# First layer in blocks of 2, 2, 2 and six times 3 chunks instead of eight times 3, with new durations and ranks for the planner of the order

## The chip, the cores and the metric

The kernel runs on one core of a Trainium2 chip. TensorE (PE) multiplies matrices into PSUM, VectorE (DVE) and ScalarE (ACT) work elementwise, SyncE (SP) issues the transfers between HBM and on-chip memory. Each engine takes its own instructions in the order in which they stand. The metric is the device time of one launch in microseconds (us), the median of several runs.

## The reference

A recurrence over time with a complex decay, then two dense layers:

```
scale = min(|a|, 0.999) / (|a| + 1e-6);  A = a * scale        # a complex: a_re, a_im
for t in range(768):                                          # 4 batches x 8 heads, D = 48
    S = A[t] * S + outer(k[t], v[t])                          # S is 48 x 48, complex
    y[t] = q[t] @ real(S)
x = y of all heads, as [3072 tokens, 384]
h = x @ w_in;   x = (max(h, 0) + alpha * min(h, 0)) @ w_out   # 384 -> 2048 -> 384
h = x @ w2_in;  out = (h - tanh(h)) @ w2_out                  # 384 -> 2048 -> 384
```

The weights and alpha arrive as float64; everything else is float32.

## The kernel before

**Recurrence.** The tokens are cut into 24 chunks of 128. Two chunks are a unit, prepared together (`unit`): ScalarE and VectorE form log|A| and its angle, TensorE sums them along the tokens (L623), and sines, exponentials and a Newton step give the factors for q and k. Then each chunk (`chunk`) turns k and q (L715, tile `kqt`), transposes them on TensorE (L726), forms the scores (L736) which VectorE masks (L738), and adds the products with the state (L754) and with v (L755) to y. The product of k and v (L765) is added to the state by VectorE (L774, in the first chunk of a batch L771) and scaled (L776). y is copied and written to HBM (`x0d`, feature by token).

**Layers.** `layer` takes one block of tokens. The first layer's block has 3 chunks, 384 tokens, so there are 8 blocks (`SIZES`, L970). The block is read back in three parts (`xf`, L801) and each part split into a high float32r half (ScalarE, L808) and a low one (VectorE, L811), tile `xt`. Then follow 16 steps of 128 hidden units. A step has 9 products into `h` (L825: three parts of 128 features, each as high by high, high by low, low by high), the activation on ScalarE and VectorE (L832, L835, tile `gg`), its split into `ghi` (ScalarE, L843) and `glo` (VectorE, L845), and 9 products into three accumulators (L856). The block's tokens are the moving columns of all 18. In the second layer (8 blocks of 384 tokens, L839, L841, L858) the activations are the weights of the second product. `h`, `gg`, `ghi` and `glo` have two buffers each, `x` (PSUM of the recurrence) three.

**Weights.** 128 hidden units of float64 weights (`weights`) come into one of two `raw` buffers. ScalarE takes magnitudes (L449), VectorE shifts and joins the words in four instructions (L35, L36, L37, L39), ScalarE copies the high float32r half (L457); the low half comes from VectorE (L472) or, for the nine weights of `PE_LO`, from TensorE by two products with the unit matrix and its negative (L466, L467), copied by ScalarE (L469).

**Order.** Nothing is issued in the order in which the code is written. `Order.add` records each operation with its engine, an estimate of its duration, its tiles and a rank (`want`). `Order.issue` then plays the program forward with these estimates: whenever an engine is free, it takes among the operations that can start by then the one with the lowest rank, if its tiles have a slot. So the durations and ranks set where each instruction stands on its engine, and nothing else; on the chip the engines wait for each other by semaphores. The ranks of the first three units are `U_WANT`, of their second chunks `C_WANT`, of later units `AHEAD` before the block that needs them, of the first layer's weights `W_WANT` (start and step). The steps of layer one have ranks 0, 1, 2, ... from the first block on, 16 to a block.

Of the kernel before, what the change touches and what calls it, by code (L numbers as in the profile page):

```python
# [18 lines left out]
def f64_words(raw):  # L19
    """Low and high words of a tile of float64 bits, the high ones also read as float32."""  # L20
    w = raw.bitcast(I32).rearrange("p (n two) -> p n two", two=2)
    wf = raw.bitcast(F32).rearrange("p (n two) -> p n two", two=2)
    return w[:, :, 0], w[:, :, 1], wf[:, :, 1]


def f64_steps(nc, raw, t):
    """float64 bits (raw(), [P, n] int64) to float32 bits in t() ([P, n] int32), on VectorE;
    t() holds the high words' magnitudes, read as float32, before.

    The high word holds sign, 11 bits of exponent and 20 of mantissa. Magnitudes outside  # L30
    float32's normal range are clamped to its ends, then the exponent's three surplus bits
    are shifted out and the low word's top three bits fill the mantissa."""
# [17 lines left out]
# High words of float64 2**-126 and of float32's largest number, read as float32.  # L50
# [4 lines left out]
def general_attention(tc, q, k, v, a_re, a_im, xd):  # L55
    """The recurrence step by step, any |a|; xd[token, (head, e)] gets y."""
# [131 lines left out]
C = 128          # tokens of a chunk of the recurrence  # L188
UN = 2 * C       # tokens of a unit: two chunks, prepared together
# [8 lines left out]

class Order:
    """Puts the program's operations in the order in which they are issued.  # L200

    An operation names its engine, about how long it takes, the tiles it reads and writes and
    those that it allocates; `want` is the rank by which an engine picks among those that can
    start. Dependences follow from the order in which the operations are added. Only shapes
    enter, so the order is the same for all inputs."""

    # from the end of one operation to the start of another that needs it, by their engines
    HOP = {("act", "dve"): 0.14, ("dve", "act"): 0.13, ("act", "act"): 0.14, ("dve", "dve"): 0.13,
           ("dve", "pe"): 0.26, ("act", "pe"): 0.26, ("pe", "dve"): 0.2, ("pe", "act"): 0.2, ("pe", "pe"): 0.0}
    COLD, WARM_UP = 3.4, 4.0        # TensorE runs at half its rate after such a pause, for that long  # L210
# [6 lines left out]
    def add(self, eng, dur, fn, want, r=(), w=(), new=(), lat=0.0, tab=None, after=()):  # L217
        i = len(self.ops)
        deps, order = set(), set(after)
        for key, tag, *parts in new:  # L220
# [4 lines left out]
            if tag not in self.FREE:  # L225
                # slots are handed out in the order in which operations are added
                if tag in self.last_new:
                    order.add(self.last_new[tag])
                self.last_new[tag] = i
# [22 lines left out]
    def chain(self):  # L252
        """ACT's functions in an order that seldom changes its table."""
# [92 lines left out]
class Fast:  # L346
    """The recurrence by chunks, from running sums of log|A| and of its angle, and the two
    MoE layers. `flag` becomes 1 if all of `a` lies where those sums are exact enough."""
# [27 lines left out]
    # -------------------------------------------------- tiles, and operations by engine  # L376
# [17 lines left out]
    # -------------------------------------------------- constants  # L394
    def constants(self):
# [24 lines left out]
        # what the general path is chosen by: sums and maxima over each unit's rows  # L420
# [5 lines left out]
    # -------------------------------------------------- weights  # L426
    def weights(self, ph, f, want):
        """float64 weights of 128 hidden units to two float32r parts."""
# [46 lines left out]
    def cvtag(self, ph, f):  # L475
        """The slot of a weight's float32 values: one of later weights' while there are some."""
        return CV[ph][f]

    def wtag(self, ph, f):
        """The slot of the weights: the second layer's begin in slots of the recurrence's."""  # L480
# [6 lines left out]
    # -------------------------------------------------- attention  # L487
    def unit(self, u, wants):
        """The running sums of a unit's two chunks. wants: rank of the operations of each chunk."""
# [30 lines left out]
        for p, sl in enumerate(halves):  # L520
# [24 lines left out]
            # logs, then 1/ar and 1/mag roughly  # L545
# [7 lines left out]
            # u = ai / ar: a Newton step on the rough 1/ar  # L553
# [7 lines left out]
            # 2 log|A|, where |A| = mag min(mag, 0.999) / (mag + 1e-6)  # L561
# [16 lines left out]
        if u % self.UPB:  # L578
            # the angle goes on from the unit before
# [3 lines left out]
        # running sums of the chunk's logs, and of the unit's angles in turns  # L583
        for what, src, keys in (("l", "sq1", sq1), ("t", "arc", arc)):
            for c in range(2):
# [15 lines left out]
                if u >= SPLIT:  # L601
# [6 lines left out]
                    dur = 0.163 * len(terms)  # L608
# [59 lines left out]
    def rank(u, what):  # L668
        """The table that ScalarE needs, and the place in the order in which it changes tables:
        each unit by itself at first, then with one unit's steps between another's."""  # L670
# [5 lines left out]
    def chunk(self, u, j, w0):  # L676
# [11 lines left out]
        # |P| = e (1 + (lc - ln e)), and its reciprocal by a Newton step  # L688
# [30 lines left out]
        for half in range(2):  # L719
            for nm in ("q", "k"):  # L720
# [6 lines left out]
                P(w0, 0.43, tr, r=[t], w=[ps], new=[(ps, "x")], after=[self.turn_pe] if half else [])  # L727
# [9 lines left out]
            self.turn_pe = P(w0, 0.86, score, r=[qT, kT], w=[ps], new=[(ps, "x")])  # L737
# [5 lines left out]
        for half in range(2):  # L743
            qT, sc = K("qT", half), K("sc", half)

            def yy(half=half, qT=qT, sc=sc):
                o = self.tile(y, "x", [128, 4, 128], psum=True) if half == 0 else T[y]
                for i in range(4):
                    h = 4 * half + i
                    m = 64 if h % 2 == 0 else D     # all rows up to the last one are written  # L750
# [7 lines left out]
        if not last:  # L758
            # the state after the chunk, in the scale of the next one's start
# [7 lines left out]
            P(w0, 0.64, kv, r=[K("kt"), K("v")], w=[ps], new=[(ps, "x")], after=[self.last_y] if self.last_y else [])  # L767
# [246 lines left out]
```

## Time and profile before

| | |
|---|---|
| timed runs (us) | 1081.90, 1082.46, 1085.41; median 1082.46 |
| profiled execution: span, first to last instruction | 1079.8 us |
| profiled execution's own time outside the span | not recorded; the median is 2.66 us above the span |
| PE busy | 1030.6 us (95%), 6584 products |
| PE weight loads busy | 990.1 us (92%) |
| DVE busy | 694.9 us (64%), 1229 instructions |
| ACT busy | 620.5 us (57%), 1234 instructions |

Times in the trace count from the span's start. A busy time is the union of an engine's instructions. Products are pipelined, so the record of one is longer than the distance to the next; what a product costs in a stream is the distance between starts. The same holds in part for VectorE. A wait is the idle time of an engine before an instruction, put down to the instruction that ended it. A float32 product is recorded as two, a float32r product or a transpose as one.

### The profile page before, as it was taken

To read this page: it belongs to the slowest core of one execution; us is meant where nothing else is said; L and a number is where in the kernel's file an instruction comes from. 1 tells how busy PE (TensorE), PEld (TensorE's weight loads), DVE (VectorE), ACT (ScalarE), POOL (GpSimd) and SP (SyncE) were. 2 spreads that over 40 slices of the span, in tenths; PEclk is the share of its full clock that TensorE was granted. 3 is DMA by queue.
4 is the path that set the end of the run, shared out by engine and by line. 5 is a ranking of instruction groups with operands and counts; after the bars stand their busy time and mean duration, and the time that the engine had idled before them with its cause. 6 is when DMAs were issued, how large, how long until landed. Compare 5 with 4: busy or idle time off the path is not lost.

```text
span 1079.8 us, 17238 instructions
## 1 busy us (share of the span) xinstructions
PE 1030.6 (95%) x6584; PEld 990.1 (92%) x6584; DVE 694.9 (64%) x1229; ACT 620.5 (57%) x1234; POOL 1.2 (0%) x8
## 2 busy tenths in 40 slices
PE   3578999999999999999999999999999999999997
PEld 1356999999999999999999999999999999999996
DVE  5998997986878876778787478843334343433332
ACT  7888679768588684868744356543334342433332
POOL 0000000000000000000000000000000000000000
PEclk9689999999999999999999999999999999999999
DMA  8556443244233333221335024210101010100000
GB/s 177 135 142 169 117 125 111 46 71 106 44 68 73 68 75 73 55 57 38 97 76 174 16 75 148 86 38 7 45 1 45 1 45 1 45 7 23 9 16 25
DMA packets 184466, 73.66 MB, mean 68 GB/s; under 512 B 146468, under 2 KB 180280, under 8 KB 184376
## 3 DMA queue, kind: packets, MB, share of 16 engines
q1 hardware_dynamic: 184376, 72.49, 26.9%
q8 instruction: 53, 0.87, 0.3%
q14 instruction: 37, 0.30, 0.1%
HBM read 58.27 MB, written 14.19 MB: 67 GB/s over the span
## 4 chain that ended last, share of the span: by engine, by line
PE 91%; ACT 5%; DVE 1%; DMA 1%; issue 1%; SPq 0%; ACTq 0%
PE h L825 37%; PE acc L858 19%; PE acc L856 18%; PE x L726 4%; PE x L736 4%; PE x L754 2%; PE x L765 2%; PE x L755 2%; PE x L623 2%; PE acc L623 1%; PE x L466 1%; DMA raw<-in_moe_w_out_dram 1%; ACT L549 0%; ACT w L457 0%; DMA a<-in_a_re_dram 0%
## 5 line engine op out<-in xcount | busy, mean ns | idle before, releaser
L825 PE MATMUL h<-xt,w 128*128 128x384 f32 x2088 | 398.2, 338 | 0.7 <-DVE gg L841 0.5
L825 PEld LDWEIGHTS h<-xt,w 128*128 128x128 f32 x2088 | 364.9, 188 | 3.1 <-issue 1.3
L845 DVE TENSOR_TENSOR glo<-gg,ghi 128x384 fp32r<-128x384 f32 x256 | 142.0, 555 | 109.8 <-ACT ghi L843 109.5
L856 PE MATMUL acc<-ghi,w 128*128 128x384 f32 x768 | 199.1, 340 | 0.0
L843 ACT CAST ghi<-gg 128x384 fp32r<-128x384 f32 x256 | 131.1, 512 | 117.9 <-DVE gg L841 44.9
L841 DVE TENSOR_TENSOR gg<-h,gg 128x384 f32<-128x384 f32 x128 | 71.3, 557 | 150.6 <-ACT gg L839 150.5
L858 PE MATMUL acc<-w,ghi 128*128 128x384 f32 x624 | 159.1, 336 | 0.2 <-ACT ghi L843 0.2
L839 ACT ACTIVATE gg<-h 128x384 f32<-128x384 f32 x128 | 63.0, 493 | 160.0 <-PE h L825 153.2
L856 PEld LDWEIGHTS acc<-ghi,w 128*128 128x128 f32 x768 | 136.7, 188 | 1.6 <-issue 1.5
L856 PE MATMUL acc<-glo,w 128*128 128x384 f32 x384 | 129.2, 336 | 0.0
L858 PEld LDWEIGHTS acc<-w,ghi 128*128 128x128 f32 x624 | 113.0, 188 | 0.5 <-ACT ghi L843 0.5
L832 ACT ACTIVATE gg<-h 128x384 f32<-128x384 f32 x128 | 62.7, 490 | 81.4 <-PE h L825 80.3
L835 DVE SCALAR_TENSOR_TENSOR gg<-gg,nal,h 128x384 f32<-128x384 f32 x128 | 78.1, 610 | 43.1 <-ACT gg L832 42.7
L858 PE MATMUL acc<-w,glo 128*128 128x384 f32 x312 | 104.8, 336 | 0.0
L856 PEld LDWEIGHTS acc<-glo,w 128*128 128x128 f32 x384 | 72.1, 188 | 0.2 <-DVE glo L845 0.2
L726 PE MATMUL x<-idt,kqt 128*96 128x128 f32 x384 | 54.7, 278 | 6.3 <-ACT w L469 3.4
L858 PEld LDWEIGHTS acc<-w,glo 128*128 128x128 f32 x312 | 58.5, 188 | 0.3 <-DVE glo L845 0.3
L726 PEld LDWEIGHTS x<-idt,kqt 128*96 128x96 f32 x384 | 42.8, 128 | 12.8 <-ACT w L469 3.6
L736 PE MATMUL x<-qT,kT 96*128 96x128 f32 x384 | 51.1, 276 | 0.0
L736 PEld LDWEIGHTS x<-qT,kT 96*128 96x128 f32 x384 | 49.3, 191 | 1.4 <-ACT w L469 0.5
L738 DVE TENSOR_TENSOR sc<-x,tri 128x512 f32<-128x512 f32 x48 | 32.9, 686 | 17.6 <-PE x L736 16.5
L728 ACT COPY qT<-x 96x512 f32<-96x512 f32 x48 | 27.7, 577 | 24.7 <-PE x L726 21.8
(171 smaller groups left out, 1298.5 us busy)
## 6 DMA issues: line engine op xcount, KB each, us to landing
raw<-in_moe_w_in_dram SPq DMA_DIRECT2D x32, 384.0 KB, 3.7
raw<-in_moe_w_out_dram SPq DMA_DIRECT2D x32, 384.0 KB, 3.8
a<-in_a_re_dram SPq DMA_DIRECT2D x24, 192.0 KB, 3.4
a<-in_a_im_dram SPq DMA_DIRECT2D x24, 192.0 KB, 4.0
k<-in_k_dram SPq DMA_DIRECT2D x24, 192.0 KB, 2.6
q<-in_q_dram SPq DMA_DIRECT2D x24, 192.0 KB, 2.9
v<-in_v_dram SPq DMA_DIRECT2D x24, 192.0 KB, 2.6
x0d<-sc SPq DMA_DIRECT2D x48, 96.0 KB, 2.2
```

Source lines behind the costliest of these rows:

```text
L726: nc.tensor.transpose(o[:, i, :], T[t][:, 4 * half + i].rearrange("p c d -> p (c d)"), self.idt)
L736: nc.tensor.matmul(o[:, i, :], T[kT][:, i, :], T[qT][:, i, :], start=True, stop=True)
L738: V(w0 - 1, 512, lambda ps=ps, sc=sc: nc.vector.tensor_tensor(self.tile(sc, "sc", [128, 4, 128]), T[ps], self.mask.unsqueeze(1).to_broadca ...
L825: nc.tensor.matmul(o, w[:, a, kt * 128:(kt + 1) * 128], x[:, b_, kt, :n], start=i == 0, stop=i == len(mms) - 1)
L832: A(E, n, lambda h=h, g=g: nc.scalar.activation(out=mt(g, "gg"), in_=T[h][:, :n], func=AF.Relu, scale=-1.0), psum=True, r=[h], w=[g], new= ...
L835: V(E, n, lambda f=f, g=g, h=h: nc.vector.scalar_tensor_tensor(T[g][:, :n], in0=T[g][:, :n], scalar=self.nal[:, f:f + 1], in1=T[h][:, :n], ...
L839: A(E, n, lambda h=h, g=g: nc.scalar.activation(out=mt(g, "gg"), in_=T[h][:, :n], func=AF.Tanh), psum=True, r=[h], w=[g], new=[(g, "gg")], ...
L841: V(E, n, lambda h=h, g=g: nc.vector.tensor_tensor(T[g][:, :n], T[h][:, :n], T[g][:, :n], op=ALU.subtract), psum=True, r=[h], w=[g])
L843: A(E, n, lambda g=g, gh=gh: nc.scalar.copy(mt(gh, "ghi", F32R), T[g][:, :n]), r=[g], w=[gh], new=[(gh, "ghi")])
L845: V(E, n, lambda g=g, gh=gh, gl=gl: nc.vector.tensor_tensor(mt(gl, "glo", F32R), T[g][:, :n], T[gh][:, :n].bitcast(F32), op=ALU.subtract), ...
L856: nc.tensor.matmul(acc[:, :n], w[:, b_, i * 128:(i + 1) * 128], gs[a][:, :n], **kw)
L858: nc.tensor.matmul(acc, gs[a][:, i * 128:(i + 1) * 128], w[:, b_, :], **kw)
```

## The change

The first layer's blocks hold 2, 2, 2, 3, 3, 3, 3, 3 and 3 chunks, nine blocks instead of eight; a block of two has 256 tokens, so its products have 256 moving columns, and its ScalarE and VectorE instructions 256 elements a partition. The second layer keeps its blocks of 384. The estimates of TensorE's operations are set anew: a float32r product of n columns by `mm_us`, the state's product of a chunk 1.36 instead of 0.64, scores 0.90 instead of 0.86. The ranks of the first units, chunks and weights are other numbers. Comments are taken out, which moves lines: what was L811 is L816, L825 is L830, L845 is L850, L856 is L861, L774 is L779 and L472 is L477. All tiles, buffers and operations are as before.

```diff
+def mm_us(n):
+
+    return max(0.112, n / 2250 + 0.0025)
...
-                    dur = 0.163 * len(terms)
+                    dur = mm_us(HD) * len(terms)
...
-                P(w0, 0.43, tr, r=[t], w=[ps], new=[(ps, "x")], after=[self.turn_pe] if half else [])
+                P(w0, 0.436, tr, r=[t], w=[ps], new=[(ps, "x")], after=[self.turn_pe] if half else [])
...
-            self.turn_pe = P(w0, 0.86, score, r=[qT, kT], w=[ps], new=[(ps, "x")])
+            self.turn_pe = P(w0, 0.9, score, r=[qT, kT], w=[ps], new=[(ps, "x")])
...
-            P(w0, 0.64, kv, r=[K("kt"), K("v")], w=[ps], new=[(ps, "x")], after=[self.last_y] if self.last_y else [])
+            P(w0, 1.36, kv, r=[K("kt"), K("v")], w=[ps], new=[(ps, "x")], after=[self.last_y] if self.last_y else [])
...
-            P(step + f, 9 * max(n, 256) / 2400, g1, r=[xt] + subs + wp, w=[h], new=[(h, "h")])
+            P(step + f, 9 * mm_us(n), g1, r=[xt] + subs + wp, w=[h], new=[(h, "h")])
...
-            P(step + f - 0.5, 9 * max(n, 256) / 2400, g2, r=[gh, gl] + wp, w=accs,
+            P(step + f - 0.5, 9 * mm_us(n) if ph == 0 else 3 * n // 128 * mm_us(self.DM), g2, r=[gh, gl] + wp, w=accs,
...
-SIZES = [3] * 8                         # chunks in a block of the first layer
-U_WANT = [-218, -242, -172]             # ranks of the first units
-C_WANT = [0, 2, 2, 4]                   # by how much a unit's second chunk is later, by unit
-AHEAD = 27                              # a later unit's rank before the block's that it is for
-W_WANT = (-34, 2.3)                     # ranks of the first layer's weights
-U_LATE = 2                              # by how much the check of the angles' range is later, in the first units
+SIZES = [2, 2, 2] + [3] * 6
+U_WANT = [-204.8, -224.2, -106.1]
+C_WANT = [-1.9, -35.6, 69.1, 6.3]
+AHEAD = 31.1
+W_WANT = (-112.8, 5.61)
+U_LATE = 29.2
```

On TensorE, where the first layer starts (`h<-xt`, the number after `w` is a weight's tile; `x<-w,idt` and `x<-w,hl` are a weight's low half), before:

```order
L466 MATMUL x<-w_291,idt 128x384
L467 MATMUL x<-w_551,hl 128x384
L466 MATMUL x<-w_790,idt 128x384
L467 MATMUL x<-w_853,hl 128x384
L466 MATMUL x<-w_790,idt 128x384
L467 MATMUL x<-w_853,hl 128x384
L825 MATMUL h<-xt,w_200 128x384 x9
L466 MATMUL x<-w_843,idt 128x384
```

And now:

```order
L628 MATMUL acc<-arc,one 128x384
L628 MATMUL acc<-arc,tri_t 128x384
L830 MATMUL h<-xt,w_200 128x256 x9
L830 MATMUL h<-xt,w_215 128x256 x9
L830 MATMUL h<-xt,w_273 128x256 x9
L861 MATMUL acc<-ghi,w_200 128x256 x2
L861 MATMUL acc<-glo,w_200 128x256
```

Two weights' low halves stood around the first step, and the second and third step behind them; now three steps follow each other, the first accumulation comes behind them, and the weights' low halves after it.

On VectorE, up to the third part of the first block's input (`xt<-xf` is the low half of an input part, `w<-raw,w` and `w<-w` are a weight's conversion, `s` the state), before:

```order
L774 TENSOR_TENSOR s<-x,s 96x384
L35 TENSOR_SCALAR w_574<-w_574 128x768
L776 TENSOR_TENSOR s<-s,g 96x384
L36 TENSOR_SCALAR w_574<-w_574 128x768
L738 TENSOR_TENSOR sc<-x,tri 128x512
L37 SCALAR_TENSOR_TENSOR w_574<-raw,w_574 128x768
L39 SCALAR_TENSOR_TENSOR w_574<-raw,w_574 128x768
L580 SCALAR_TENSOR_TENSOR arc<-carry,arc 1x384
L472 TENSOR_TENSOR w_770<-w_574,w_770 128x768
L738 TENSOR_TENSOR sc<-x,tri 128x512
L35 TENSOR_SCALAR w_790<-w_790 128x768
L811 TENSOR_TENSOR xt<-xf,xt 128x384
```

And now:

```order
L779 TENSOR_TENSOR s<-x,s 96x384
L632 TENSOR_SCALAR lc<-acc 128x384
L781 TENSOR_TENSOR s<-s,g 96x384
L37 SCALAR_TENSOR_TENSOR w_559<-raw,w_559 128x768
L35 TENSOR_SCALAR w_571<-w_571 128x768
L39 SCALAR_TENSOR_TENSOR w_559<-raw,w_559 128x768
L779 TENSOR_TENSOR s<-x,s 96x384
L36 TENSOR_SCALAR w_571<-w_571 128x768
L743 TENSOR_TENSOR sc<-x,tri 128x512
L781 TENSOR_TENSOR s<-s,g 96x384
L585 SCALAR_TENSOR_TENSOR arc<-carry,arc 1x384
L816 TENSOR_TENSOR xt<-xf,xt 128x256
```

The two additions to the state of the second unit's chunks now have one weight's instructions between them, and the first input part follows soon after.

## Rows read from the trace of the kernel before

**Rows 1.** The page: span, busy us with share, the last chain by engine.

```profile
span 1079.8 us, 17238 instructions
...
PE 1030.6 (95%) x6584; PEld 990.1 (92%) x6584; DVE 694.9 (64%) x1229; ACT 620.5 (57%) x1234; POOL 1.2 (0%) x8
...
PE 91%; ACT 5%; DVE 1%; DMA 1%; issue 1%; SPq 0%; ACTq 0%
```

**Rows 2.** Busy us of PE, PEld, DVE, ACT, POOL; then clock, DMA, GB/s.

```profile
0.00:20.00 20.00, 5.54 (x8) 2.34 (x8) 10.05 (x34) 12.91 (x29) 1.20 (x8) 1.00 0.83 158
20.00:104.00 84.00, 57.26 (x364) 40.39 (x365) 77.16 (x124) 69.06 (x129) 0.00 (x0) 0.82 0.65 157
104.00:136.00 32.00, 31.99 (x237) 28.77 (x235) 29.94 (x50) 22.71 (x41) 0.00 (x0) 0.95 0.42 114
136.00:660.00 524.00, 523.88 (x3620) 507.87 (x3621) 402.72 (x710) 358.88 (x717) 0.00 (x0) 1.00 0.33 78
```

**Rows 3.** What TensorE waited for in 0:104: total us, times, longest.

```profile
PE acc L623 <- DVE sq L562: 13.8, 1, 13.8
```

**Rows 4.** Timeline at the first product: start, length, what [idle before].

```profile
103.77 0.56 DVE L811 TENSOR_TENSOR xt<-xf,xt 128x384 fp32r<-128x384 f32 x1 [0.32 <-ACT xt L808]
...
104.06 0.68 PE L825 MATMUL h<-xt,w 128*128 128x384 f32 x2
```

**Rows 5.** A stretch of the second layer, columns as in rows 2.

```profile
700.00:1000.00 300.00, 300.00 (x1724) 300.00 (x1724) 112.89 (x210) 108.18 (x228) 0.00 (x0) 1.00 0.07 23
```

**Rows 6.** TensorE's timeline, score products and what follows.

```profile
117.77 1.05 PE L736 MATMUL x<-qT,kT 96*128 96x128 f32 x8
118.66 1.04 PE L726 MATMUL x<-idt,kqt 128*96 128x128 f32 x8
```

**Rows 7.** VectorE's timeline at the fifth step of block 0.

```profile
133.48 0.60 DVE L835 SCALAR_TENSOR_TENSOR gg<-gg,nal,h 128x384 f32<-128x384 f32 x1
134.00 0.55 DVE L36 TENSOR_SCALAR w<-w 128x768 int32<-128x768 int32 x1
134.47 0.55 DVE L559 TENSOR_SCALAR arc<-arc 128x768 f32<-128x768 f32 x1
134.94 0.55 DVE L845 TENSOR_TENSOR glo<-gg,ghi 128x384 fp32r<-128x384 f32 x1
```

**Rows 8.** TensorE's timeline, a weight's pair and what follows it.

```profile
133.83 0.91 PE L466 MATMUL x<-w,idt 128*128 128x384 f32 x2
...
134.84 0.43 PE L754 MATMUL x<-qT,s 96*64 96x128 f32 x4
```

**Rows 9.** What VectorE waited for in 17:136: total us, times, longest.

```profile
DVE s L774 <- PE x L765: 2.0, 2, 1.8
DVE sc L738 <- PE x L736: 1.9, 3, 1.0
DVE w L472 <- ACT w L457: 1.4, 2, 0.8
DVE w L35 <- ACT w L449: 1.0, 2, 0.8
```

**Rows 10.** VectorE's timeline up to the third addition to a state.

```profile
81.97 0.94 DVE L715 TENSOR_TENSOR kqt<-k,cs 128x768 f32<-128x768 f32 x1
82.83 0.68 DVE L738 TENSOR_TENSOR sc<-x,tri 128x512 f32<-128x512 f32 x1
83.44 0.55 DVE L776 TENSOR_TENSOR s<-s,g 96x384 f32<-96x384 f32 x1
83.90 0.95 DVE L715 TENSOR_TENSOR kqt<-q,cs 128x768 f32<-128x768 f32 x1
...
88.40 0.55 DVE L774 TENSOR_TENSOR s<-x,s 96x384 f32<-96x384 f32 x1 [1.75 <-PE x L765]
```

**Rows 11.** What VectorE waited for in 140:172.

```profile
DVE glo L845 <- ACT ghi L843: 2.5, 3, 1.9
...
DVE gg L835 <- ACT gg L832: 1.0, 3, 0.4
```

## The prediction, on record before the changed kernel ran

> **What bounds the kernel now.** I read the page first, then busy time by stretches, then the waits of TensorE and of VectorE, then the places where the first layer starts. The page gives a span of 1079.8 us of which TensorE is busy 1030.6, and the chain that ended last lies on TensorE for 91% [rows 1]. Lost on TensorE are thus 49.2 us. By stretches they lie at the start: 14.5 us of the first 20, 26.7 of the next 84, none between 104 and 136, 0.1 between 136 and 660 [rows 2]; the rest lies behind 660, most of it the drain at the end. So from 104 us on the kernel ends when TensorE has done its list, and a change can move the end in two ways: by the length of that list, or by how early TensorE gets going without a break.
>
> What holds TensorE up in the first 104 us is VectorE. It is busy 77.2 of the 84 us between 20 and 104, and 29.9 of the 32 after that [rows 2]; TensorE's longest wait there is for a VectorE result [rows 3]. VectorE takes the float64 weights apart, prepares the recurrence and splits the activations, and TensorE gets what falls off. The engines meet at about 136 us: after it VectorE has 121 us free in 524 while TensorE has none [rows 2]. The first product of layer one starts at 104.06, right behind the last of the three splits of its input, VectorE's at 103.77, which had waited for ScalarE's half [rows 4].
>
> **The change, part by part.**
>
> *Length of TensorE's list.* Six chunks go through layer one as three blocks of 256 columns instead of two of 384. A block is 16 hidden steps of 18 products, so 864 narrow products stand for 576 wide ones. A wide one costs 0.174 us: 1724 in 300.00 us of the second layer, where nothing waits [rows 5]. A narrow float32r product is not in this trace. If the time goes with the columns it is 0.116, and 864 x 0.116 = 100.2 against 576 x 0.174 = 100.2: no difference. From below: eight products with weights of the same 128 columns follow each other in 118.66 - 117.77 = 0.89 us, 0.111 each [rows 6], so weight loads alone permit that rate: 864 x 0.111 = 96.1, 4.1 us less. From above: 384 columns at the full 2.4 GHz take 0.160, and if the other 0.014 is a fixed charge per product, a narrow one costs 0.107 + 0.014 = 0.121, 104.3 in all, 4.1 us more. I take 0.116, the middle, and keep both ends.
>
> The Trainium skill, in "TensorE: Matmul & The Clock Gate", section "Back-to-back issue gap", gives N/2.4 + 2.5 ns for warm products: 162.5 ns at 384 columns, 109 at 256. The trace has 174 for the first, so it does not bear the rule out there, and the measurement decides. By the page's figure the narrow products would take an estimated 94.3 us, 5.9 less than the wide ones do here.
>
> The rest of the list is unchanged: the recurrence has the same products, and its new estimates (the state's product 1.36 instead of 0.64, for instance) alter the order only.
>
> *When TensorE gets going.* In the new order the last VectorE split ahead of the first product is 5 instructions nearer the start: 3 of 384 columns become 256 (-0.13 each), 2 of the quick 768-column kind and 3 of the full 768-column kind are no longer ahead of it. By the distance between starts a full 768 costs 0.86 (81.97 to 82.83), a 384 one 0.46 to 0.47 (83.44 to 83.90) [rows 10], a quick 768 one 0.47 (134.00 to 134.47) [rows 7]: 0.4 + 0.9 + 2.6 = 3.9 us. The first product should start at about 100.2 instead of 104.06, and four of TensorE's small weight products move from before it to after it. This by itself does not move the end. VectorE is still behind, and what counts is the point at which VectorE's work ahead exceeds TensorE's by most, since TensorE's idle time adds up to that lead.
>
> I count both lists to the same kind of point. In before the fifth step of block 0 is where TensorE is last held up; the fifth low half of its activations (VectorE) starts at 134.94 [rows 7] and TensorE has no gap from then on. In the new order the lead stays high much longer. To the twelfth step of its block 0, against that fifth step, VectorE has 13 fewer of 384 columns, 7 more quick 768, 10 more full 768, and 30 of 256 columns. The last kind I estimate from the steps between lengths: (0.86 - 0.47)/384 per column, so 0.47 - 0.13 = 0.34, and for those that read PSUM 0.52 (133.48 to 134.00) - 0.13 = 0.39 [rows 7]; half of each is 11.0. Together -6.1 + 3.3 + 8.6 + 11.0 = 16.8 us. TensorE between the same points has 225 narrow products (26.1) for 81 wide (14.1), and 4 more weight pairs at 134.84 - 133.83 = 1.0 less a switch, say 0.95 [rows 8]: 12.0 + 3.8 = 15.8, with 0.3 for two products of the next unit's sums 16.1. The recurrence ahead of both points is the same, product for product. The lead is 16.8 - 16.1 = 0.7 us larger, so TensorE loses 0.7 us more if VectorE idles as much as before. A count to the fifteenth step gives 0.6. The earlier start is eaten up: in a narrow block each step brings TensorE 2.1 us of work instead of 3.1, while each weight costs VectorE the same.
>
> *VectorE's own waits.* In the stretch from 17 to 136 us VectorE waited 2.0 us for the state's product in its later chunks, 1.9 for scores, 1.4 + 1.0 for ScalarE's weight copies and magnitudes [rows 9]. The longest is at the third addition of a state: from the start of the turned keys at 81.97 to the addition at 88.40 are 6.43 us, 1.75 of them waiting [rows 10]. The new order has nine instructions from the one to the other: four full 768, a mask of 0.61 (82.83 to 83.44) and four of 0.47, 5.9 us in all. The product that it waits for has about the same work ahead of it on TensorE, so 0.5 us of waiting should be left: 1.2 saved. Bounds are all 2.0 us saved and none.
>
> *What else is added.* Sixteen more steps in layer one mean more, shorter ScalarE and VectorE instructions: on VectorE 48 x (0.39 + 0.34) against 32 x (0.52 + 0.47), 3.4 us more. All but the part counted above lies after 136 us, where VectorE is free 121 us of 524; if that cover went, it would cost those 3.4. SP issues three more loads and three more stores of a block, on a DMA share of 0.33 [rows 2]. Weights and units are reordered within the same two raw buffers, so SP's waits for them move with VectorE, which is in the count above.
>
> Sum: 0 (products) + 0.7 (lead) - 1.2 (waits) = -0.5 us, span 1079.3. The timed median is 1082.46, 2.7 above the profiled span; I keep that distance: **1082.0 us**.
>
> **The rivals.**
>
> *A: VectorE's waits fall away for the most part.* For it: 6.3 us of waits are listed [rows 9], and the planner now knows the real lengths. Against it: 2.4 of them are for ScalarE's part of the weights, and the first weights stand in the same order as before. With 5 us gone: 1082.5 + 0.7 - 5 = 1078.2.
>
> *B: narrow products cost less than their share,* 0.111, with everything else as forecast: 1082.0 - 4.1 = 1077.9. For it: the row at 0.111. Against it: no row shows a float32r product that quick. The page's figure would give an estimated 1082.0 - 5.9 = 1076.1.
>
> *C: slower, by the steps of blocks 0 and 1 held in a ring.* Each step goes TensorE, ScalarE, VectorE, ScalarE, VectorE, TensorE, with two buffers for each intermediate. With 384 columns TensorE has 3.1 us of other work per step, with 256 it has 2.1. Between 140 and 172 us VectorE waited 2.5 + 1.0 us for ScalarE in about ten steps [rows 11], harmless then since TensorE was ahead. In the new order TensorE is not ahead until the end of block 0: 15 steps at 0.35 are 5.2 us that come through to the end: 1082.0 + 5.2 = 1087.2. It decides as soon as VectorE's idle time between the first product and the end of block 0 exceeds what it saved before. For it: the lead is flat from the first to the fifteenth step, so any VectorE wait there is TensorE's. Against it: the planner fills such gaps with weight work where it has some.
>
> *D: a fixed charge per product,* 0.121: 1082.0 + 4.1 = 1086.1.
>
> That the change does not do what it says is excluded by the order: 256-column products stand there, and the first split is earlier.
>
> **How the numbers follow.** A measurement of this kernel tells about 0.3%, 3.2 us, from no change. Forecast 0.40 (its own range 1079.3 to 1085.7), A 0.22, B 0.08, C 0.24, D 0.06. A and B are faster by more than 0.3%: 0.30; the forecast is the same: 0.40; C and D are slower: 0.30. The range has to reach into A and B below and C and D above; C could be half as large again, A likewise: 1075 to 1090.
>
> **What would show it.** The first product of layer one near 100 us rather than 104. Products of 256 columns 0.116 us apart; 0.111 or 0.121 would be B or D. Gaps on TensorE between the first product and the end of block 0, with VectorE's low halves named as releaser, that before did not have; their sum minus the time saved at the start is C. VectorE's waits for the state's product shorter than 2.0 us. After block 2, TensorE without gaps. I am wrong if TensorE's idle time before block 1 changes by more than 3 us, or if it waits again between 200 and 650 us.

## The result, and the profile after

The changed kernel takes 1090.62 us (median of four runs, 1089.66 to 1091.14) against 1082.40 for before beside it: ratio 1.0070, 95% interval 1.0052 to 1.0087. It is slower by 8.2 us, just beyond the upper end of the stated range (1090), and the forecast of no change was wrong.

The page after, lines as in [rows 1]:

```profile
span 1089.3 us, 17924 instructions
...
PE 1036.9 (95%) x6872; PEld 994.7 (91%) x6872; DVE 691.8 (64%) x1264; ACT 617.3 (57%) x1272; POOL 1.2 (0%) x8
...
PE 82%; DVE 7%; ACT 6%; issue 2%; DMA 2%; SPq 0%; ACTq 0%; DVEq 0%
```

Busy time by stretches after, as in [rows 2]:

```profile
0.00:20.00 20.00, 5.12 (x8) 2.20 (x8) 10.07 (x33) 13.00 (x29) 1.20 (x8) 1.00 0.83 158
20.00:104.00 84.00, 59.49 (x376) 43.19 (x376) 76.14 (x125) 68.95 (x130) 0.00 (x0) 0.80 0.61 149
104.00:136.00 32.00, 31.20 (x244) 27.53 (x245) 31.51 (x58) 26.15 (x52) 0.00 (x0) 1.00 0.58 163
136.00:660.00 524.00, 520.98 (x3855) 503.71 (x3854) 398.98 (x727) 352.44 (x738) 0.00 (x0) 1.00 0.32 75
```

TensorE's idle time falls by 2.2 us between 20 and 104, rises by 0.8 up to 136, and is 3.0 between 136 and 660 where it was 0.1. The prediction named waits between 200 and 650 as a sign that it was wrong; 2.2 of the 3.0 lie there. The waits of TensorE between 136 and 660 (engine, line, line waited for: total us, times, longest):

```profile
PE h L830 <- DVE gg L840: 2.2, 4, 0.9
PE acc L861 <- DVE glo L850: 0.5, 1, 0.5
PE acc L861 <- ACT ghi L848: 0.2, 1, 0.2
```

The last narrow product starts at 264.6. The same stretch cut there, and the two longest waits:

```profile
136.00:265.00 129.00, 128.17 (x1126) 123.53 (x1125) 111.96 (x221) 105.01 (x239) 0.00 (x0) 1.00 0.40 87
265.00:660.00 395.00, 392.81 (x2731) 380.19 (x2730) 287.02 (x508) 247.43 (x500) 0.00 (x0) 1.00 0.30 71
...
307.88 1.83 PE L830 MATMUL h<-xt,w 128*128 128x384 f32 x9 [0.89 <-DVE gg L840]
...
453.36 1.83 PE L830 MATMUL h<-xt,w 128*128 128x384 f32 x9 [0.78 <-DVE gg L840]
```

Only 0.8 us of the waits behind 136 are in the stretch of the narrow blocks; 2.2 come in the wide blocks behind them. Both long ones stand before the third of three hidden steps in a row. `h` has two buffers, and the profile names as what ended the wait the activation (L840), which is the last to read one.

The start after (start, length, engine, line, what; in brackets the idle time before it and what ended it), against [rows 4]:

```profile
98.19 0.69 PE L830 MATMUL h<-xt,w 128*128 128x256 f32 x2
...
99.57 0.39 ACT L813 CAST xt<-xf 128x256 fp32r<-128x256 f32 x1
...
100.02 0.62 PE L830 MATMUL h<-xt,w 128*128 128x256 f32 x3 [1.14 <-ACT xt L813]
...
100.64 0.42 DVE L816 TENSOR_TENSOR xt<-xf,xt 128x256 fp32r<-128x256 f32 x1
...
101.11 1.80 PE L830 MATMUL h<-xt,w 128*128 128x256 f32 x13 [0.47 <-DVE xt L816]
...
104.37 1.29 PE L830 MATMUL h<-xt,w 128*128 128x256 f32 x9 [1.47 <-DVE gg L840]
```

The first product starts 5.9 us earlier, but on two of the three input parts. It waits 1.14 and 0.47 us for the third, then 1.47 for an activation: 3.1 of the 5.9 are given back within eight microseconds.

The end after:

```profile
1075.64 1.75 PE L830 MATMUL h<-xt,w 128*128 128x384 f32 x9
1077.48 0.49 ACT L844 ACTIVATE gg<-h 128x384 f32<-128x384 f32 x1 [4.49 <-PE h L830]
1078.01 0.56 DVE L846 TENSOR_TENSOR gg<-h,gg 128x384 f32<-128x384 f32 x1 [4.42 <-ACT gg L844]
1078.60 0.51 ACT L848 CAST ghi<-gg 128x384 fp32r<-128x384 f32 x1 [0.62 <-DVE gg L846]
...
1079.16 0.62 PE L863 MATMUL acc<-w,ghi 128*128 128x384 f32 x2 [1.78 <-ACT ghi L848]
...
1081.84 0.52 PE L863 MATMUL acc<-w,glo 128*128 128x384 f32 x1
```

The second layer's code, tiles and products are those of before, but the planner has put its steps in another order. The last ones read, with h for the nine products of a hidden step and A for its accumulation:

```
before:  h13 A12 h14 A13 h15 A14 A15
after:   h12 h13 h14 A12 A13 A14 h15 A15
```

In before, A14 stood between h15 and A15 and covered the activation of step 15 (a wait of 0.2 us was left). Now nothing does. Ahead of that the steps come in threes, three hidden steps and then three accumulations, where in before they alternate.

Where the 9.5 us of span went is seen best from three places, read off each profiled execution (start of the product named, us; layer two is the third less the second); the experiments of the next section stand beside them:

| kernel | first product | last of layer one | last product | layer two |
|---|---|---|---|---|
| before | 104.06 | 670.94 | 1072.38 | 401.44 |
| after | 98.19 | 676.40 | 1081.84 | 405.44 |
| e_tail | 97.89 | 675.70 | 1077.37 | 401.67 |
| e_l2dur | 98.24 | 677.09 | 1078.75 | 401.66 |
| e_sizes_only | 103.44 | 681.32 | 1083.02 | 401.70 |
| e_late | 103.59 | 674.66 | 1074.87 | 400.21 |
| e_less_before | 104.09 | 670.95 | 1072.37 | 401.42 |
| e_less_after | 96.64 | 675.69 | 1080.14 | 404.45 |
| e_narrow_ranks | 98.93 | 673.72 | 1074.88 | 401.16 |
| e_new_ranks | 101.90 | 669.93 | 1070.92 | 400.99 |

Layer one ends 5.5 us later, and layer two takes 4.0 longer. (In e_late nine more products of layer two stand ahead of the last one of layer one, so 1.6 us of its layer two are counted with layer one.)

Of the 5.5 us, 1.9 are idle time of TensorE: 4.5 less ahead of its first product of layer one, 6.4 more behind it. In the other 3.6 it is recorded as busy; the price of the narrow products is 1.5 of them (see e_late). A product's record is longer than the distance to the next, so a short hold does not show as idle time, and the remaining 2.1 were not traced to a cause.

### The profile page after: what moved, and what is told of

Read it like the earlier page. It is cut to its first block, busy times and chain, and to the rows that moved or that the text cites. A ratio compares the mean times of both kernels' runs of the same rounds, so it can differ in the third digit from the quotient of the medians.

```text
span 1089.3 us, 17924 instructions
## 1 busy us (share of the span) xinstructions
PE 1036.9 (95%) x6872; PEld 994.7 (91%) x6872; DVE 691.8 (64%) x1264; ACT 617.3 (57%) x1272; POOL 1.2 (0%) x8
## 4 chain that ended last, share of the span: by engine, by line
PE 82%; DVE 7%; ACT 6%; issue 2%; DMA 2%; SPq 0%; ACTq 0%; DVEq 0%
PE h L830 31%; PE acc L863 19%; PE acc L861 15%; PE x L731 4%; PE x L741 4%; PE x L759 2%; PE x L770 2%; PE x L760 2%; PE x L628 1%; DMA raw<-in_moe_w_out_dram 1%; PE acc L628 1%; PE x L471 1%; DVE gg L840 1%; DMA xf<-x1d 1%; ACT ghi L848 1%
## 5 line engine op out<-in xcount | busy, mean ns | idle before, releaser
L830 PE MATMUL h<-xt,w 128*128 128x384 f32 (+1 forms) x2232 | 393.7, 327 | 5.8 <-DVE gg L840 3.7
L830 PEld LDWEIGHTS h<-xt,w 128*128 128x128 f32 x2232 | 367.6, 188 | 10.1 <-DVE gg L840 5.2
L850 DVE TENSOR_TENSOR glo<-gg,ghi 128x384 fp32r<-128x384 f32 (+1 forms) x272 | 144.7, 533 | 114.4 <-ACT ghi L848 113.8
L848 ACT CAST ghi<-gg 128x384 fp32r<-128x384 f32 (+1 forms) x272 | 134.2, 494 | 128.9 <-PE acc L863 49.8
L861 PE MATMUL acc<-ghi,w 128*128 128x384 f32 (+1 forms) x864 | 203.4, 322 | 0.5 <-ACT ghi L848 0.5
L844 ACT ACTIVATE gg<-h 128x384 f32<-128x384 f32 x128 | 62.8, 491 | 163.4 <-PE h L830 159.0
L861 PEld LDWEIGHTS acc<-ghi,w 128*128 128x128 f32 x864 | 146.9, 188 | 3.2 <-issue 1.9
L861 PE MATMUL acc<-glo,w 128*128 128x384 f32 (+1 forms) x432 | 137.4, 318 | 0.7 <-DVE glo L850 0.7
L840 DVE SCALAR_TENSOR_TENSOR gg<-gg,nal,h 128x384 f32<-128x384 f32 (+1 forms) x144 | 81.4, 566 | 49.4 <-ACT gg L837 49.1
L837 ACT ACTIVATE gg<-h 128x384 f32<-128x384 f32 (+1 forms) x144 | 64.9, 451 | 64.1 <-PE h L830 62.0
L861 PEld LDWEIGHTS acc<-glo,w 128*128 128x128 f32 x432 | 81.3, 188 | 1.5 <-DVE glo L850 1.5
```

Of the source, the lines that this page charges most:

```text
L830: nc.tensor.matmul(o, w[:, a, kt * 128:(kt + 1) * 128], x[:, b_, kt, :n], start=i == 0, stop=i == len(mms) - 1)
L837: A(E, n, lambda h=h, g=g: nc.scalar.activation(out=mt(g, "gg"), in_=T[h][:, :n], func=AF.Relu, scale=-1.0), psum=True, r=[h], w=[g], new= ...
L840: V(E, n, lambda f=f, g=g, h=h: nc.vector.scalar_tensor_tensor(T[g][:, :n], in0=T[g][:, :n], scalar=self.nal[:, f:f + 1], in1=T[h][:, :n], ...
L844: A(E, n, lambda h=h, g=g: nc.scalar.activation(out=mt(g, "gg"), in_=T[h][:, :n], func=AF.Tanh), psum=True, r=[h], w=[g], new=[(g, "gg")], ...
L848: A(E, n, lambda g=g, gh=gh: nc.scalar.copy(mt(gh, "ghi", F32R), T[g][:, :n]), r=[g], w=[gh], new=[(gh, "ghi")])
L850: V(E, n, lambda g=g, gh=gh, gl=gl: nc.vector.tensor_tensor(mt(gl, "glo", F32R), T[g][:, :n], T[gh][:, :n].bitcast(F32), op=ALU.subtract), ...
```

## The experiments

Times are medians; ratios are to before, with 95% intervals.

**e_tail, e_l2dur: the second layer.** The first moves nine products, the second puts layer two's old durations back:

```diff
-            P(step + f, 9 * mm_us(n), g1,
+            P(step + f - (3 if (ph, j, f) == (1, 7, KF - 1) else 0), 9 * mm_us(n), g1,
```
```diff
-            P(step + f, 9 * mm_us(n), g1,
+            P(step + f, 9 * (mm_us(n) if ph == 0 else n / 2400), g1,
...
-            ... 9 * mm_us(n) if ph == 0 else 3 * n // 128 * mm_us(self.DM), g2,
+            ... 9 * (mm_us(n) if ph == 0 else n / 2400), g2,
```

> The changed kernel with one move: in the last block of layer two the last hidden step's nine products are issued ahead of the two accumulations before them, so that two accumulations (3.1 us) lie between them and the last accumulation that needs them. Theory of the uncovered end: the 1.78 us that TensorE waits for the last step's activations goes, and with it the half rate of the last seven products (0.24 instead of 0.174, 0.5 us), so 1090.6 - 2.3 = 1088.3. Rival (the loss lies wholly in the first layer and the end is drained by something else, for example the output's copies and stores): 1090.6, unchanged.

> The changed kernel, with the planner's durations of layer two's steps alone put back to columns / 2400 (1.44 us a step instead of 1.56); the order up to the end of layer one is the same, product for product. Theory of the durations: they bunched layer two's steps in threes, which cost 1.3 us along the layer and 2.6 at the end, so 1090.6 - 3.9 = 1086.7. Rival (the order in layer two is harmless, all is lost in the narrow blocks): 1090.6.

e_tail: 1087.05, 1.0047 (1.0033 to 1.0061). e_l2dur: 1087.93, 1.0048 (1.0034 to 1.0062). They are 3.6 and 2.7 us under the changed kernel. At the end of e_tail:

```profile
1071.28 1.75 PE L830 MATMUL h<-xt,w 128*128 128x384 f32 x9
...
1077.37 0.34 PE L863 MATMUL acc<-w,glo 128*128 128x384 f32 x1
```

No wait is left there, and layer two takes 401.67 us again. So one move gives back 3.8 of the 4.0 us. e_l2dur, which undoes the bunching in threes too, is no faster, but that does not make the bunching free. Distances between starts in layer two, counted from the last product of layer one:

| | before | e_l2dur | e_tail | after |
|---|---|---|---|---|
| 100th to 2200th product behind it (us) | 365.79 | 365.80 | 366.73 | 367.21 |
| the last nine products (us) | 2.31 | 2.30 | 1.57 | 4.79 |

The first row is 365.5 to 365.8 in every run with the old durations of layer two and 366.5 to 367.2 in every run with the new ones, so the bunched order costs 0.7 to 1.4 us along the layer. e_tail keeps most of that loss and makes up for it at the end, which its move covers better than before did. Of the changed kernel's 4.0 us, 1.4 are lost along the layer between these two places and 2.5 in the last nine products, close to what I had read from the traces beforehand (1.3 and 2.6).

**Which part: undoing one of three, doing one of three.** The blocks (`SIZES`), the durations and the ranks of the diff, each put back alone and each made alone:

> The changed kernel with eight blocks of 3 chunks again; the new durations and the new ranks stay. Theory of the durations (second layer's order) plus narrow blocks: what is left is layer two's 3.9 us, so 1082.4 + 3.9 = 1086.3, and the 4.3 us of the narrow blocks (1.7 of products, the rest waits in blocks 0 to 2) are gone. Theory that durations and ranks alone do it: 1090. Theory that the narrow blocks alone do it: 1082.4.

> The changed kernel with the planner's old durations (state's product 0.64, a step at columns / 2400 but at least 256 of them); the blocks of 2, 2, 2 and the new ranks stay. Theory of both: without layer two's 3.9 us, 1086.7, if the first layer's order is as good as with the new durations. Theory of the narrow blocks alone: 1090 or more. Theory of the durations alone: 1082.4 to 1084.

> The changed kernel with the old ranks: blocks of 2, 2, 2 and new durations. Theory that parts fit together: the first product later than 98 us (104 to 108) and layer two's 3.9 us still lost: 1092 to 1096. Theory of parts that add up: 1090.6 - 29.9 = 1060.7.

> The kernel before with the blocks of 2, 2, 2 alone. Theory of the narrow blocks held in the ring: the first product near 104 us as before, then about 5 us of waits in the narrow blocks that before did not have, and 1.4 us of products: 1088.8. Theory of parts that add up: 1082.4 - 8.3 = 1074.1.

> The kernel before with the new durations alone. Theory: layer two's steps are bunched in threes and the last one is uncovered, 3.9 us, with the first layer much as before: 1086.3. If the first layer also starts later, more: up to 1092. Theory of parts that add up: 1082.4 - 13.4 = 1069.

> The kernel before with the new ranks alone. Theory that the ranks suit only the blocks and durations they were set with: the first layer starts late, beyond 115 us instead of 104, as it did when either of the others was put back, and the kernel takes 1094 to 1104. Rival, that the three parts add up (undoing the blocks cost 8.3 us, undoing the durations 13.4, so the ranks would cost 8.2 + 8.3 + 13.4 = 29.9): 1112.

| blocks | durations | ranks | run | us | ratio | first product |
|---|---|---|---|---|---|---|
| new | new | new | after | 1090.62 | 1.0070 | 98.19 |
| old | new | new | e_no_sizes | 1098.94 | 1.0162 | 131.30 |
| new | old | new | e_no_durs | 1103.95 | 1.0202 | 131.72 |
| new | new | old | e_no_ranks | 1097.45 | 1.0156 | 115.62 |
| new | old | old | e_sizes_only | 1092.28 | 1.0099 | 103.44 |
| old | new | old | e_durs_only | 1100.35 | 1.0174 | 116.67 |
| old | old | new | e_ranks_only | 1098.80 | 1.0167 | 132.98 |

All six lie above the changed kernel. My expectations of 1086 for e_no_sizes and e_durs_only and of 1086.7 for e_no_durs missed by 13 to 17 us, and those that the parts add up by 13 to 37. e_ranks_only fell into its 1094 to 1104; e_no_ranks missed by 1.5 and e_sizes_only by 3.5. The mechanism shows in the last column: in five of the six the first product comes 12 to 29 us later than in before. So no price of a part can be read from undoing it, only from a kernel in which the rest fits. Layer two's time sorts the runs: with its old durations 401.4 to 401.7 (e_ranks_only, e_sizes_only, e_no_durs), with the new ones 403.7 to 405.4, each time with a wait of 1.77 or 1.78 us ahead of the last accumulation.

e_sizes_only is the cleanest of them: start and layer two as before, layer one 10.4 us later. TensorE's waits there between 136 and 172 us:

```profile
PE x L628 <- DVE hl L601: 0.7, 1, 0.7
PE h L830 <- DVE w L477: 0.6, 1, 0.6
PE h L830 <- DVE gg L840: 0.5, 2, 0.3
PE acc L861 <- ACT ghi L848: 0.5, 1, 0.5
```

They are many and small, for a unit's sums, a weight, and the step's own activations. I read this as a step of 2.1 us of products covering less of everything; no run shows that by itself. These waits are 2.3 of the 10.4 us. In all, 5.5 are idle time up to the end of layer one, 1.63 of it in one wait at 455.1, in a wide block; in the other 4.9 TensorE is recorded as busy.

**e_late: the narrow products by themselves.** `SIZES = [3] * 6 + [2] * 3` in before.

> The kernel before with its narrow blocks at the end of layer one instead of its start: blocks of 3, 3, 3, 3, 3, 3, 2, 2, 2 chunks, old ranks and durations, so that the start is as before and the narrow blocks lie where TensorE is ahead of nothing it needs. It prices the narrow products by themselves. Theory that they cost their columns and a little: 864 x 0.1176 - 576 x 0.174 = 1.4 us, 1083.5. Theory of a dearer step (the switch from a hidden step to an accumulation comes 48 x 2 times instead of 32 x 2): 3 us, 1085. Rival, that narrow blocks wait for their activations wherever they stand: 1089, as with the blocks of 2, 2, 2 alone.

1085.80, 1.0032 (1.0020 to 1.0043): 3.5 us above before, by the interval 2.2 to 4.7. That fits the theory of a dearer step (3 us); 1.4 us alone is too little, and the rival of 1089 is out. The 864 narrow products here stand 0.1174 us apart on the mean (distances under 1.5 times the median, which leaves out 19 here and 43 in the changed kernel), in the changed kernel 0.1177: 864 x 0.1177 - 576 x 0.174 = 1.5 us. The last product is 2.5 us later than in before, so about 1.0 are waits. They hardly lie in the narrow blocks: of 1.1 us more idle time behind 136 us, 0.2 are in them, 0.5 in a wide block ahead of them and 0.4 at the start of layer two.

**e_less_before, e_less_after: is it VectorE?** The last step of the weights' conversion in layer one on 32 of 768 columns, all else in place:

```diff
-        lambda: V.scalar_tensor_tensor(t(), in0=f64_words(raw())[0], scalar=29, in1=t(),
+        lambda: V.scalar_tensor_tensor(t()[:, :n], in0=f64_words(raw())[0][:, :n], scalar=29, in1=t()[:, :n],
...
-f64_steps(nc, raw_, lambda: T[cv])
+f64_steps(nc, raw_, lambda: T[cv], 32 if ph == 0 else None)
```

> The changed kernel with less VectorE work at the same places: the last step of the float64 conversion of layer one's weights takes 32 of 768 columns (the low word's three bits are left out in the others), 0.95 us down to an estimated 0.1, 16 times, 8 of them ahead of the first product. Theory that VectorE's amount of work sets TensorE's time in the narrow blocks: the first product 6 to 7 us earlier, and at the end of the third block 7 to 13 us saved: 1078 to 1084. Rival, that the narrow steps wait for the chain through ScalarE and the two buffers of each kind: the start is earlier but the narrow blocks give it back, no more than 2 us saved at the end of the third block: 1088.6 or more.

> The kernel before with the same cut in VectorE's work (9 of the 16 steps lie ahead of its first product, 12 ahead of the place where TensorE is last held up). Theory that VectorE's amount of work sets TensorE's time up to 135 us: up to 12 x 0.85 = 10.2 us saved, at least half of it: 1072 to 1077. If TensorE's time in that stretch is set by loads or ScalarE instead: 1080 or more.

e_less_before: 1081.70, 0.9994 (0.9985 to 1.0004). e_less_after: 1089.56, 1.0063 (1.0045 to 1.0082), not told apart from the changed kernel's 1.0070. Busy time by stretches of e_less_before, and its first product:

```profile
20.00:104.00 84.00, 57.78 (x364) 41.28 (x365) 71.18 (x125) 69.05 (x129) 0.00 (x0) 0.82 0.65 157
104.00:136.00 32.00, 32.00 (x237) 28.70 (x235) 27.79 (x50) 22.62 (x41) 0.00 (x0) 0.95 0.43 114
```
```profile
104.09 1.90 PE L825 MATMUL h<-xt,w 128*128 128x384 f32 x6
```

VectorE has 8.1 us less to do in these 116 us (77.16 + 29.94 before), and the first product stands where it stood. The amount of VectorE's work on the weights does not set the start. The chain of waits of before, which I had not followed there (start, length, what):

```profile
98.54 0.59 ACT sc L780
99.13 0.42 ACT cs L646
...
99.94 0.53 ACT f L649
100.47 0.80 ACT w L449
101.27 0.51 ACT cs L650
101.78 0.41 ACT cs L646
102.19 0.73 ACT w L457
...
102.96 0.45 PE x L467
103.41 0.65 PE x L466 x2
104.05 0.17 PE x L467
104.22 0.84 PE h L825 x3
```

The last five microseconds before the first step are ScalarE's queue and then TensorE's own; from 60 us on the chain does not touch VectorE at all. TensorE's last wait before 448 us is there too, and it is for ScalarE's copy of a weight:

```profile
102.96 0.45 PE L467 MATMUL x<-w,hl 128*128 128x384 f32 x1 [1.88 <-ACT w L457]
```

In e_less_after the first product does come earlier, at 96.64 instead of 98.19, but layer one ends only 0.7 us earlier.

**e_act_before, e_act_after, e_act_sizes: is it ScalarE?** The magnitudes of layer one's weights on 32 of 768 columns:

```diff
-            nc.scalar.activation(out=t.bitcast(F32), in_=f64_words(raw_())[2], func=AF.Abs)
+            n = 32 if ph == 0 else 768
+            nc.scalar.activation(out=t[:, :n].bitcast(F32), in_=f64_words(raw_())[2][:, :n], func=AF.Abs)
+            if n < 768:
+                nc.gpsimd.memset(t[:, n:].bitcast(F32), 1.0)
```

> The kernel before with less ScalarE work at the same places: the first step of the float64 conversion of layer one's weights (magnitudes of the high words) takes 32 of 768 columns on ScalarE, 0.8 us down to an estimated 0.2, 16 times; the idle GpSimd fills the rest with a constant, so the weights' values are wrong there. Theory that the start is a chain through ScalarE and TensorE: three of these steps lie on the chain itself between 30 and 102 us with 1.65 us, and more queue ahead of it, so the first product starts 1.2 to 4 us before 104 and the kernel ends as much earlier, 1078 to 1081. Rival, that the recurrence's own steps and loads set the start: not over 0.5 us, 1082.

> The changed kernel with the same cut in ScalarE's work. Theory of the chain through ScalarE: 2 to 5 us less, 1086 to 1089, the first product earlier and the waits between 98 and 106 us shorter. Rival: not over 1 us, as with VectorE's work.

> The kernel before with the blocks of 2, 2, 2 alone and the same cut in ScalarE's work. Theory that the narrow steps there wait for weights, which come through ScalarE: of the 5.6 us lost between 136 and 172 at least 3 go, beside what the start gains: 1086 to 1089. Rival, that they wait for the activations of their own steps: those 5.6 us stay, 1090 to 1092.

e_act_before: 1080.91, 0.9990 (0.9980 to 1.0000), first product at 102.21. Busy time of its engines:

```profile
20.00:104.00 84.00, 58.60 (x373) 41.62 (x373) 78.49 (x125) 65.51 (x131) 3.36 (x4) 0.82 0.65 158
```

ScalarE has 3.6 us less to do there, and the first product comes 1.85 earlier, about what lay on the chain. e_act_after: 1089.44, 1.0067 (1.0050 to 1.0084), not told apart from the changed kernel. e_act_sizes: 1091.77, 1.0097 (1.0080 to 1.0113), its layer one ending at 681.08 against 681.32: the narrow steps' waits are not for weights from ScalarE. In e_act_after the first product even comes later, at 99.67. ScalarE's work counts in part for the start of before, and VectorE's work on the weights does not; neither sets the time of the changed kernel. What does set its start was not found.

**e_new_ranks, e_ranks_b, e_ranks_c, e_narrow_ranks: blocks or ranks.** Layer two as in e_l2dur, sets of ranks as listed in the expectations, the first three with eight blocks of 3.

> Eight blocks of 3 chunks, the new durations in the recurrence and layer one, columns / 2400 in layer two, and ranks set anew for this (first units -286, -287.8, -262.2; second chunks later by 45.2, -330.4, -367.6, 12.4; ahead 24.4; weights -9.7 and 0.54 a weight; check 257.7 later). Theory that what the changed kernel lost is the narrow blocks' products (3 us) and layer two (2.7 to 3.5 us), and that its start is worth having: 1090.6 - 6 = 1084.6 with a start like its own, 1081 or less if the better fit holds. Rival, that the start of before is better than any of this kind: 1086 or more.

> Eight blocks of 3, the durations as in e_new_ranks, and another set of ranks (first units -452.5, -453.6, -93.2; second chunks later by 319.8, -166.4, -546.7, 7.0; ahead 28.4; weights -98.8 and 0.68 a weight; check 216.9 later). Theory that what is left to gain lies in the waits of layer one behind 136 us: 1080.5 to 1081.5. Rival, that the start of before can't be bettered by ranks: 1082.5 or more.

> As e_ranks_b with a third set (first units -109.1, -464.0, -174.2; second chunks later by -18.9, -313.4, -225.6, 6.8; ahead 28.2; weights -11.4 and 0.26 a weight; check 544.6 later): the same, 1081 to 1082; rival 1082.5 or more.

> The changed kernel's blocks of 2, 2, 2 with columns / 2400 as layer two's durations and another set of ranks (first units -277.8, -345.5, -122.9; second chunks later by -167.1, -88.3, 116.6, 7.1; ahead 28.3; weights -238.6 and 14.26 a weight; check 266 later). Theory that the narrow blocks cost by themselves (products 1.5 us, waits of a shorter step 2 to 3): 1085.5 to 1088, that is 3 to 5 us above eight blocks of 3 with ranks set alike (1082.7). Theory that only the changed kernel's ranks were at fault: 1082 to 1084.

e_new_ranks: 1082.73, 1.0005 (0.9995 to 1.0015). e_ranks_b: 1084.43, 1.0017 (1.0004 to 1.0031). e_ranks_c: 1082.30, 0.9997 (0.9987 to 1.0007). e_narrow_ranks: 1084.86, 1.0030 (1.0018 to 1.0042). Blocks of 3 with the new durations in the recurrence and layer one, and with ranks set for them, come to the time of before in two of three sets; narrow blocks with ranks set for them come 2.7 us above it, about as much as e_late. Against e_l2dur (1.0048), which has the same durations and blocks, other ranks are worth 2 to 3 us, and layer one ends 3.4 us earlier. None of these beats before by what can be told.

## Why the prediction was wrong

*The step that failed: "The rest of the list is unchanged ... alter the order only", costed at nothing.* The new durations are used in layer two as well, and I compared the orders only up to the end of the first layer's early blocks. The new order bunches the steps and leaves the last activation uncovered: 4.0 us between the last product of layer one and the last of all, of which one move of nine products gives back 3.8. With that move the time is 1087.05, inside the range, but 5 us above the forecast and outside the forecast's own 1079.3 to 1085.7. So this was not the only step that failed.

*The second: the sum stops at the start of layer one, "After block 2, TensorE without gaps".* Its terms for the start, +0.7 - 1.2, came near: TensorE's idle time up to 136 us fell by 1.0. But layer one ends 5.5 us later. Between 136 us and the end of layer one TensorE idles 2.9 us more, most of it behind block 2, and up to that end it is recorded as busy for 3.6 us more, 1.5 of them the narrow products. The sum had 0 for the products and no term for the rest.

*That -0.5 is near -1.0 is luck.* VectorE's waits did not shrink and its work did not set the start (both below). The point to which I counted in before, 134.94, is not where TensorE was last held up either: [rows 2] has no idle time between 104 and 136, and the last wait is the one at 102.96 shown above.

*Length of TensorE's list: 0, measured +1.5.* 0.1177 us a product lies within my bounds of 0.111 and 0.121. Rival B falls. The 109 ns that the prediction takes from the Trainium skill ("TensorE: Matmul & The Clock Gate", section "Back-to-back issue gap") are not borne out either: here 118. That section calls its formula the gap of an isolated product, and the prediction used it for a stream.

*"What holds TensorE up in the first 104 us is VectorE": refuted.* I inferred it from a busy share of 92%, and the +0.7 of the lead rests on it. Taking 8.1 us of its work on the weights away left the first product where it was. [Rows 4] had the hint: the last VectorE split waited for ScalarE.

*First product "near 100 us": the split I counted to came at 100.64,* 3.1 earlier where I had 3.9; the count of instructions was near. But an earlier start is worth what follows it without a wait, and 3.1 us of waits followed.

*VectorE's waits, -1.2: did not happen.* Its wait for the state's product between 17 and 136 us, 2.0 in [rows 9], is after:

```profile
DVE s L779 <- PE x L770: 2.6, 2, 2.4
```

*Rival C: right in direction, not in place or size.* TensorE does wait for activations in the narrow blocks. But C's 5.2 us were to be gaps in block 0 less the time saved at the start. The gaps there sum to 3.5, all before 107 us, and 4.5 us of idle time were saved, so by C's own measure nothing was lost. That its 1087.2 is close to e_tail's 1087.05, the changed kernel with its end covered, is luck. Nor is it only a ring: waits for sums and weights stand beside those for activations in e_sizes_only. How the 4 us of layer one beside the products divide into the blocks' own waits and the ranks, the runs bound only: with other ranks 2.7 of them go. A third buffer for `gg`, `ghi` and `glo`, which would test the ring alone, was not tried.

## What to carry to other kernels

Where a planner sets the order, a new estimate acts wherever the operation occurs: compare the order to the last instruction, and look at what covers the last step of the last loop. Two runs with the same time need not agree inside: look at the stretches before concluding that a part costs nothing. A busy share of 92% does not make an engine the bound; follow the chain of waits through the stretch, and price an engine's work by what lies on that chain. Ranks tuned for one set of sizes and durations are part of it, so an edit can't be priced by undoing it alone.

## What was not expected of the hardware

The wait at the end cost more than its 1.78 us. TensorE's granted clock after (busy us, then the clock, DMA share, GB/s):

```profile
1070.00:1077.00 7.00, 7.00 (x41) 1.00 0.01 2
1077.00:1079.70 2.70, 0.92 (x5) 1.00 0.00 0
1079.70:1082.00 2.30, 2.30 (x8) 0.50 0.07 25
```

After a stretch in which it was busy 0.92 of 2.70 us, TensorE did its last eight products at the lower of its two levels, 1.2 GHz. From 1079.16 to 1081.84 it starts nine products, 2.68 us for eight distances. e_less_after ends in the same order with the same wait, and there the clock stayed up:

```profile
1078.39 0.62 PE L863 MATMUL acc<-w,ghi 128*128 128x384 f32 x2 [1.77 <-ACT ghi L848]
...
1080.14 0.34 PE L863 MATMUL acc<-w,glo 128*128 128x384 f32 x1
```
```profile
1079.00:1080.00 1.00, 1.00 (x7) 1.00 0.00 0
```

There the eight distances take 1.75 us, so the lower clock cost 0.9. Of the six profiled kernels that end on this wait, it fell in two (after and e_durs_only) and stayed up in four, one execution each; what decides it is not shown.

Before has such a stretch at the start of layer one. Behind the waits of 0.67 and 1.88 us the granted clock was 0.50 from 105 to 107 us, and the first products stood 0.32 us apart instead of 0.174. In the changed kernel it stayed at 1.00 from 98 to 110 us, through waits of 1.14, 0.47 and 1.47 us. Its start thus gains about 1 us that the prediction did not have, an estimate from the seven distances at 0.32 us.
